# One ring of four double banks for the attention's PSUM tiles

## The chip, the cores and the metric

The kernel runs on one core of a Trainium2 chip. The metric is the device time of one execution in microseconds (us); lower is better. Inputs are the reference's arrays, the output is one float32 array of 8 x 576 x 512.

## What is computed

Attention over 8 batches and 8 heads with queries pooled by two, then a block that mixes tokens and channels:

```python
q_pool = q.reshape(B, H, S // 2, 2, D).mean(axis=3)          # 8, 8, 576, 64
scores = (1.0 / np.sqrt(D)) * np.matmul(q_pool, k.transpose(0, 1, 3, 2))
attn = np.exp(scores - np.max(scores, axis=-1, keepdims=True))
attn = attn / (np.sum(attn, axis=-1, keepdims=True) + 1e-09)
x = np.matmul(attn, v).transpose(0, 2, 1, 3).reshape(B, 576, 512)
theta = x @ w_theta
y = einsum('ts,bsd->btd', w_tok_r, x * cos(theta)) + einsum('ts,bsd->btd', w_tok_i, x * sin(theta))
u = x + y
out = u + np.maximum(u @ w_ch, 0.0)
```

q, k and v have 1152 rows of 64 per head.

## The kernel before

There are two parts, each with its own PSUM pool. The first makes x for all batches (attention), the second does the rest, batch by batch. The change touches the first part.

Attention goes over 32 pairs of heads (`NPAIR`), which overlap: while pair i is in its main stage, pair i+2 is in its maximum pass and pair i+3 is being prepared. The work of a pair:

- **Preparation** (`prep_t`, `prep_hi`, `prep_lo`, `prep_tail`; L252 to L292). TensorE transposes the keys and the pooled queries into a PSUM tile `pt` of two banks (L265), in two groups: g = 0 with six key blocks, g = 1 with the queries and three key blocks. ScalarE copies it, rounded, to `hi` (L281); VectorE writes the rest `lo` = `pt` - `hi` (L292), so that products can be made in three fast terms. For g = 1 ScalarE also copies the last 64 queries of both heads into a matrix `tail` (L288).
- **Maximum pass** (`maxpass`, L305 and L312). In twelve steps TensorE writes 128 queries by 384 keys for both heads to a tile `pm` (L305, 2 matmuls), and VectorE reduces it to a maximum (L312). The last 64 queries of both heads go together (`max_tail`): three matmuls fill the two banks of `px` (L322), and a fourth, of 128 columns, for which `px` has no room, goes to spare columns of another tile (L328; here called py's columns). VectorE reduces `px` (L331) and then py's columns (L332). `max_nm` (L337) and `max_row` (L342 to L344) turn the maxima into the row `mT`, which DMAs bring to `nmr` for the subtraction.
- **Main stage** (`escore`, L371 and L374). For each half u of the queries and each of nine key blocks TensorE makes a score tile `pe` (8 matmuls: four terms, two heads), and ScalarE writes its exponential to `pc` (L374). GpSimd adds these up (`ssum`, L383).
- **Output** (`av`, L392 and L399). 36 matmuls of `pc` and `vn` go to bank 0 of a tile `pa`, and ScalarE copies that to `xu`. The sums of the exponentials over the partitions go to bank 1 of the tile `pmt` (`norm_sum`, L408), and what follows divides by them.

Each PSUM tile of this part has two of the eight banks (`bank2`). In before there are two kinds with two tiles each: "e" for `pe` and `pa`, "m" for `pm`, `pt`, `px`, `pmt` and the transposed weights `pwt`. A new tile of a kind takes the place of the one two before it and waits until that has been read. The layer that records the program puts the semaphores in: instructions of different engines on one PSUM tile are kept in the order of the code, also where two only read it, and also, as the first matmul of L408 shows with the copy `mT` (L344), where they use different banks of it.

The order of the work on each engine is written out by hand: `plan` gives each step a position (18 score tiles of a pair are 18 units; `MAX_AT`, `AV_AT`, `W_AT` and `PLAN` are such positions), ties go by a priority, and each engine runs its instructions in that order. At `AV_AT` a pair has two bursts (`burst`): the first with the preparation of g = 1 for pair i+2, `max_row` and `av` for u = 0, the second with `tail_prep` and `av` for u = 1. In the second burst of before, the code has first the transposes of pair i+3, then `max_tail` of pair i+2, whose py's columns go to spare columns of the tile `pt` just transposed, then `hi` and `lo` of pair i+3, then `av`. Nine positions of a pair (`W_AT`) advance a generator by one step each; it narrows the weights of the second part, mostly on VectorE (L525 to L540), some steps on ScalarE and GpSimd.

Of the kernel before, what the change touches and what calls it, by code (L numbers as in the profile page):

```python
# [9 lines left out]
F32 = mybir.dt.float32  # L10
# [4 lines left out]
ALU = mybir.AluOpType  # L15
AX = mybir.AxisListType
# [1 line left out]
EPS = 1e-9  # L18
TAIL = 8
PC_BUFS = 14  # L20
MAX_AT = (-24.9, -23.65, -22.55, -20.85, -19.55, -18.8, -15.55, -14.35, -13.5, -11.6, -10.2, -9.15)
SS_LAG = 4.5
AV_AT = (10.35, 19.25)
W_FIRST = (9.45, 9.5, 9.85, 10.5, 12.75, 18.0, 18.6, 19.25, 20.45)
W_AT = (9.45, 9.5, 9.85, 10.5, 12.75, 18.0, 18.6, 19.25, 20.45)
W_LAST = (9.4, 10.2, 11.0, 11.8, 12.6, 13.4, 14.2, 15.0, 15.8, 16.6, 17.4, 18.2, 19.0, 19.8, 20.6, 21.4, 22.2, 23.0, 23.8, 24.6)
W_END = 30
PRO = ((-34.75, -25.8, -18.2), (-6.0, -5.0, 3.15), (3.75,))
MAX_AT0 = (-25.75, -25.25, -24.75, -24.25, -24.15, -23.25, -22.0, -21.95, -21.75, -21.25, -20.75, -20.25)
MAX_AT1 = (-18.1, -16.8, -16.1, -15.35, -14.7, -14.0, -13.3, -12.6, -11.7, -10.3, -9.8, -9.0)  # L30
PLAN = {
    "load_q": -44.55,
    "load_k": -43.2,
    "pool_q": -35.35,
    "load_max": -7.6,
    "load_v": -7.0,
    "max_nm": -8.85,
    "norm_spread": 29.0,
    "norm_load": 29.15,
    "norm_recip": 37.5,  # L40
    "norm_save": 37.6,
    "norm_bcast": 37.7,
# [2 lines left out]
}  # L45
MAN = ("PE", "Activation", "DVE", "Pool", "SP")
BANKS = {}
PAIRS = {"e": 2, "m": 2}
BANKS2 = {"h": 1, "t": 1, "m": 4, "r": 2}
MAN2 = ("PE", "Activation", "DVE", "Pool", "SP")  # L50
ENG2 = {'xlo0': 'vector', 'zlo0': 'gpsimd', 'xlo': 'gpsimd', 'zlo': 'gpsimd', 'ulo': 'vector'}
# [40 lines left out]
def pooled_attention_moe_kernel(  # L92
# [11 lines left out]
    nc = tc.nc  # L104
# [83 lines left out]
    with ExitStack() as p1:  # L188
# [63 lines left out]
        def prep_t(i, g):  # L252
            st = state[i]
            kn = st["kn"]
            pt = st["pt", g] = bank2("m", f"pt{g}_{i}")
            if g == 0:
                srcs = [[kn[:, t] for t in range(3 * n, 3 * n + 3)] for n in range(2)]
            else:
                qp = st["qp"]
                srcs = [[qp[:, t] for t in range(5)], [qp[:, 5]] + [kn[:, t] for t in (6, 7, 8)]]  # L260
            for n in range(2):
                c = 0
                for src in srcs[n]:
                    R = src.shape[0]
                    nc.tensor.transpose(  # L265
                        out=pt[:, n, c : c + R],
                        in_=src.rearrange("p h d -> p (h d)"),
                        identity=ident[0:R, 0:R],
                    )
                    c += R  # L270
# [12 lines left out]
        def prep_tail(i):  # L283
            st = state[i]
            tl = st["tail"] = tails[i % 2]
            c = QP - HT
            for hs in HEADS:
                nc.scalar.copy(tl[hs, hs], st["pt", 1][hs, 1, c : c + HT])  # L288
# [7 lines left out]
        def maxpass(i):  # L296
            st = state[i]
            hi = st["hi"]
            mx = st["mx"] = sml.tile([P, KT, 3], F32, tag="mx", name=f"mx{i}")
            W = 3 * P  # L300
            for j in range(4):
                for g in range(3):
                    pm = bank2("em"[g % 2] if i == 0 else "m", f"pm{i}_{j}{g}")
                    for h, hs in enumerate(HEADS):
                        nc.tensor.matmul(  # L305
                            pm[:, h, 0:W],
                            hi[hs, Q0 + j * P : Q0 + (j + 1) * P],
                            hi[hs, K0[3 * g] : K0[3 * g] + W],
                            start=True,
                            stop=True,  # L310
                        )
                    nc.vector.tensor_reduce(  # L312
                        mx[:, j : j + 5 : 4, g : g + 1], pm[:, :, 0:W], AX.X, ALU.max
                    )
                    yield

        def max_tail(i, pt):
            st = state[i]
            hi, tl, mx = st["hi"], st["tail"], st["mx"]
            pm = bank2("m", f"px{i}")  # L320
            for n, c, k, w in ((0, 0, 0, 4), (1, 0, 4, 2), (1, 2 * P, 6, 2)):
                nc.tensor.matmul(  # L322
                    pm[:, n, c : c + w * P], tl, hi[:, K0[k] : K0[k] + w * P], start=True, stop=True
                )
            st["pm", 0] = pm
            if pt is None:
                pt = bank2("m", f"py{i}")
            nc.tensor.matmul(  # L328
                pt[:, 0, 3 * P :], tl, hi[:, K0[8] : K0[8] + P], start=True, stop=True
            )  # L330
            nc.vector.tensor_reduce(mx[:, 8, 0:2], pm, AX.X, ALU.max)  # L331
            nc.vector.tensor_reduce(mx[:, 8, 2:3], pt[:, 0, 3 * P :], AX.X, ALU.max)  # L332
# [5 lines left out]

        def max_row(i):
            st = state[i]  # L340
            px = bank2("m", f"pmt{i}")
            nc.tensor.transpose(out=px[0:KT, 0, 0:P], in_=st["nm"], identity=ident)  # L342
            mT = st["mT"] = sml.tile([KT, P], F32R, tag="mT", name=f"mT{i}")
            nc.scalar.copy(mT, px[0:KT, 0, 0:P])  # L344
            return px
# [36 lines left out]
            first = st["pc"][u, 0] if kt == 1 else st["ss", u]  # L382
            nc.gpsimd.tensor_tensor(st["ss", u], first, st["pc"][u, kt], ALU.add)  # L383

        def av(i, u):
            st = state[i]
            if u == 0:
                st["xu"] = nrm.tile([P, 2, HALF], F32, tag="xu", name=f"xu{i}", bufs=3)
            pa = bank2("e", f"pa{i}_{u}")
            for kt in range(KT):  # L390
                for h, hs in enumerate(HEADS):
                    nc.tensor.matmul(  # L392
                        pa[hs, 0, 0:HALF],
                        st["vn"][:, h, kt, :],
                        st["pc"][u, kt][:, h, :],
                        start=(kt == 0),
                        stop=(kt == KT - 1),
                    )
            nc.scalar.copy(st["xu"][:, u, :], pa[:, 0, 0:HALF])  # L399
# [56 lines left out]
        def burst(i, u):  # L456
            if u == 0:
                if i + 2 < NPAIR:
                    prep_all(i + 2, 1)
                px = max_row(i + 1) if i + 1 < NPAIR else bank2("m", f"pmt{i}")  # L460
                av(i, u)
                if i > 0:
                    norm_sum(i - 1, px)
            else:
                tail_prep(i)
                av(i, u)

        def prep_all(i, g):
            if g == 0:
# [5 lines left out]
                prep_tail(i)  # L475

        def tail_prep(i):
            more = i + 3 < NPAIR
            if more:
                prep(i + 3)  # L480
                prep_t(i + 3, 0)
            if i + 2 < NPAIR:
                max_tail(i + 2, state[i + 3]["pt", 0] if more else None)
            if more:
                prep_hi(i + 3, 0)
                prep_lo(i + 3, 0)
# [9 lines left out]
        def weights():  # L496
# [494 lines left out]
```

## Time and profile before

| what | value |
|---|---|
| median of 3 timed runs | 1419.48 us (1417.49 to 1420.95) |
| the profiled execution | 1416.78 us, its span 1414.8 us |
| mean granted TensorE clock | 0.992 |
| busy share of the span: TensorE, its weight loads | 96%, 77% |
| VectorE, ScalarE, GpSimd | 61%, 52%, 64% |

The profile is of one execution. PE is TensorE's matmuls and PEld its weight loads, DVE is VectorE, ACT ScalarE, POOL GpSimd, SP the queue of the DMAs. Attention ends near 920 us. Times in rows are us from the span's start; "idle before" is how long an engine stood before a row and what released it. Matmul durations overlap: the next pair of matmuls starts before the last has drained, so the distance of two starts tells more than a duration.

### The profile page before, as it was taken

To read this page: it belongs to the slowest core of one execution; us is meant where nothing else is said; L and a number is where in the kernel's file an instruction comes from. 1 tells how busy PE (TensorE), PEld (TensorE's weight loads), DVE (VectorE), ACT (ScalarE), POOL (GpSimd) and SP (SyncE) were. 2 spreads that over 40 slices of the span, in tenths; PEclk is the share of its full clock that TensorE was granted. 3 is DMA by queue.
4 is the path that set the end of the run, shared out by engine and by line. 5 is a ranking of instruction groups with operands and counts; after the bars stand their busy time and mean duration, and the time that the engine had idled before them with its cause. 6 is when DMAs were issued, how large, how long until landed. Compare 5 with 4: busy or idle time off the path is not lost.

```text
span 1414.8 us, 29922 instructions
## 1 busy us (share of the span) xinstructions
PE 1352.8 (96%) x12178; PEld 1086.1 (77%) x12178; DVE 862.2 (61%) x1143; ACT 730.6 (52%) x1250; POOL 911.4 (64%) x672
## 2 busy tenths in 40 slices
PE   5999999999999999999999999999999999999998
PEld 4667676766676767767776766688999999999998
DVE  5866676777577767766687666355362553536442
ACT  2556465655555655556565655465444544445431
POOL 2789888978798889889898888834232413232210
PEclk7999999999999999999999999999999999999999
DMA  5224343434342443324343421231111211111111
GB/s 127 74 75 126 85 111 84 119 85 116 86 125 69 108 122 106 94 83 125 84 111 86 119 80 51 79 122 38 35 38 34 60 50 34 38 35 44 28 31 38
DMA packets 130906, 111.66 MB, mean 79 GB/s; under 512 B 95040, under 2 KB 95424, under 8 KB 130768
## 3 DMA queue, kind: packets, MB, share of 16 engines
q1 hardware_dynamic: 130592, 109.28, 28.0%
q8 instruction: 96, 1.57, 0.5%
q0 software_dynamic: 176, 0.46, 0.1%
q14 instruction: 42, 0.34, 0.1%
HBM read 88.29 MB, written 21.27 MB: 77 GB/s over the span
## 4 chain that ended last, share of the span: by engine, by line
PE 67%; DVE 15%; ACT 10%; DMA 3%; issue 3%; POOL 1%; SPq 0%; ACTq 0%; POOLq 0%; DVEq 0%
PE pa L392 16%; PE pe L371 16%; PE py L821 11%; PE pth L743 7%; PE pr L860 5%; DVE mx L312 5%; ACT pc L374 4%; PE pm L305 3%; PE pt L265 3%; PE pmt L408 2%; DMA kn<-in_k_dram 2%; DVE wf L532 1%; PE pxn L731 1%; DVE ws L530 1%; DVE lo L292 1%
## 5 line engine op out<-in xcount | busy, mean ns | idle before, releaser
L383 POOL TENSOR_TENSOR ss<-ss,pc 128x576 f32<-128x576 f32 x384 | 558.1, 1453 | 98.2 <-ACT pc L374 75.9
L312 DVE TENSOR_REDUCE mx<-pm 128x2 f32<-128x768 f32 x384 | 343.9, 950 | 134.8 <-PE pm L305 134.4
L374 ACT ACTIVATE pc<-pe 128x576 f32<-128x576 f32 x576 | 371.2, 652 | 102.2 <-PE pe L371 84.2
L392 PE MATMUL pa<-pc,vn 128*64 128x288 f32 x2304 | 293.5, 409 | 0.3 <-ACT pc L374 0.3
L794 POOL TENSOR_TENSOR Z<-ab,Z 128x512 fp32r<-128x512 f32 x40 | 52.2, 1305 | 306.0 <-ACT Z L790 277.8
L392 PEld LDWEIGHTS pa<-pc,vn 128*64 128x64 f32 x2304 | 159.7, 137 | 110.7 <-ACT pc L374 4.8
L821 PE MATMUL py<-wtk,Z 128*128 128x288 f32 x1728 | 241.7, 297 | 0.0
L821 PEld LDWEIGHTS py<-wtk,Z 128*128 128x128 f32 x1728 | 233.2, 189 | 1.3
L371 PE MATMUL pe<-hi 64*128 64x288 f32 x1152 | 203.1, 349 | 14.9 <-ACT pc L374 6.5
L371 PEld LDWEIGHTS pe<-hi 64*128 64x128 f32 x1152 | 108.3, 184 | 92.9 <-ACT pc L374 57.9
L371 PE MATMUL pe<-hi,lo 64*128 64x288 f32 x1152 | 170.8, 293 | 0.0
L371 PE MATMUL pe<-lo,hi 64*128 64x288 f32 x1152 | 170.8, 293 | 0.0
L371 PE MATMUL pe<-nmr,oner 64*128 64x288 f32 x1152 | 169.5, 290 | 0.0
L305 PE MATMUL pm<-hi 64*128 64x384 f32 x768 | 138.1, 359 | 14.6 <-DVE mx L312 8.6
L371 PEld LDWEIGHTS pe<-lo,hi 64*128 64x128 f32 x1152 | 109.8, 187 | 0.0
L371 PEld LDWEIGHTS pe<-hi,lo 64*128 64x128 f32 x1152 | 109.1, 186 | 0.0
L371 PEld LDWEIGHTS pe<-nmr,oner 64*128 64x128 f32 x1152 | 109.0, 185 | 0.0
L292 DVE TENSOR_TENSOR lo<-pt,hi 128x768 fp32r<-128x768 f32 x64 | 67.6, 1057 | 66.9 <-ACT hi L281 66.9
L860 PEld LDWEIGHTS pr<-us,wch 128*128 128x128 f32 x768 | 104.5, 188 | 2.0
L860 PE MATMUL pr<-us,wch 128*128 128x288 f32 x768 | 105.8, 295 | 0.0
L281 ACT CAST hi<-pt 128x768 fp32r<-128x768 f32 x64 | 56.2, 878 | 91.5 <-DVE mx L332 74.3
L383 POOL TENSOR_TENSOR ss<-pc,pc 128x576 f32<-128x576 f32 x64 | 93.8, 1466 | 3.0 <-ACT pc L374 3.0
(105 smaller groups left out, 1652.7 us busy)
## 6 DMA issues: line engine op xcount, KB each, us to landing
qn<-in_q_dram SPq DMA_DIRECT2D x32, 576.0 KB
kn<-in_k_dram SPq DMA_DIRECT2D x64, 288.0 KB
vn<-in_v_dram SPq DMA_DIRECT2D x32, 576.0 KB
dn<-ro SPq DMA_DIRECT2D x64, 144.0 KB
xd<-xu SPq DMA_DIRECT2D x32, 288.0 KB
xT<-xd SPq DMA_DIRECT2D x8, 1152.0 KB
out_dram<-on SPq DMA_DIRECT2D x23, 192.0 KB
out_dram<-on SPq DMA_DIRECT2D x23, 128.0 KB
```

The source lines that it names most:

```text
L281: nc.scalar.copy(hi, src)
L292: nc.vector.tensor_tensor(lo, src, hi.bitcast(F32), ALU.subtract)
L305: nc.tensor.matmul(pm[:, h, 0:W], hi[hs, Q0 + j * P : Q0 + (j + 1) * P], hi[hs, K0[3 * g] : K0[3 * g] + W], start=True, stop=True,)
L312: nc.vector.tensor_reduce(mx[:, j : j + 5 : 4, g : g + 1], pm[:, :, 0:W], AX.X, ALU.max)
L371: nc.tensor.matmul(pe[:, h, 0:HALF], w[hs], x[hs], start=(n == 0), stop=(n == 3))
L374: nc.scalar.activation(pcs[u, kt], pe[:, :, 0:HALF], AF.Exp, scale=SC)
L383: nc.gpsimd.tensor_tensor(st["ss", u], first, st["pc"][u, kt], ALU.add)
L392: nc.tensor.matmul(pa[hs, 0, 0:HALF], st["vn"][:, h, kt, :], st["pc"][u, kt][:, h, :], start=(kt == 0), stop=(kt == KT - 1),)
L743: nc.tensor.matmul(th, xs[c][:, j * P : (j + 1) * P], ws[:, c], start=(n == 0), stop=(n == 11))
L794: engine("zlo", b).tensor_tensor(Z[1], t, Z[0].bitcast(F32), ALU.subtract)
L821: nc.tensor.matmul(st["py", c, u][:, 0:HALF], Z[zi][:, c * P : (c + 1) * P], wtk[wi][:, kw, u * HALF : (u + 1) * HALF], start=(i == 0 and ...
L860: nc.tensor.matmul(pr[u][:, 0:HALF], wch[wi][:, c, e * P : (e + 1) * P], st["us", ui][:, c, u * HALF : (u + 1) * HALF], start=(n == 0), st ...
```

## The change

There is one kind of tile, "e", with four tiles in a ring (the same eight banks): every tile waits for the one four before it, whichever of `pe`, `pm`, `pt`, `px`, `pmt`, `pwt` and `pa` that is. `tail` is copied from `hi` in SBUF rather than from `pt`; `hi` holds the same rounded values. In the second burst `hi` and `lo` of pair i+3 come right behind the transposes in the code, then the tile `pa` of u = 1 is taken, py's columns go to its bank 1, and `av` writes its bank 0. Positions of many steps move by small amounts. Of these the three that the prediction names: the weight step at 10.5 goes to 9.896, ahead of the first burst; the one at 19.25, which stood behind the second burst, is at 19.246, ahead of it (19.269); and the one at 20.45 goes to 19.685.

```diff
-MAX_AT = (-24.9, -23.65, -22.55, -20.85, -19.55, -18.8, -15.55, ...)
+MAX_AT = (-24.792, -23.501, -21.909, -20.702, -19.409, -18.667, -15.437, ...)
-AV_AT = (10.35, 19.25)
+AV_AT = (10.348, 19.269)
-W_AT = (9.45, 9.5, 9.85, 10.5, 12.75, 18.0, 18.6, 19.25, 20.45)
+W_AT = (9.455, 9.493, 9.833, 9.896, 12.767, 17.992, 18.599, 19.246, 19.685)
...
-PAIRS = {"e": 2, "m": 2}
+PAIRS = {"e": 4}
...
         def prep_t(i, g):
-            pt = st["pt", g] = bank2("m", f"pt{g}_{i}")
+            pt = st["pt", g] = bank2("e", f"pt{g}_{i}")
...
         def prep_tail(i):
-            c = QP - HT
+            c = Q0 + SQ - HT
             for hs in HEADS:
-                nc.scalar.copy(tl[hs, hs], st["pt", 1][hs, 1, c : c + HT])
+                nc.scalar.copy(tl[hs, hs], st["hi"][hs, c : c + HT].bitcast(F32))
...
         def maxpass(i):
-                    pm = bank2("em"[g % 2] if i == 0 else "m", f"pm{i}_{j}{g}")
+                    pm = bank2("e", f"pm{i}_{j}{g}")
...
         def max_tail(i, pt):
-            pm = bank2("m", f"px{i}")
+            pm = bank2("e", f"px{i}")
...
             nc.tensor.matmul(
-                pt[:, 0, 3 * P :], tl, hi[:, K0[8] : K0[8] + P], start=True, stop=True
+                pt[:, 1, 0:P], tl, hi[:, K0[8] : K0[8] + P], start=True, stop=True
             )
             nc.vector.tensor_reduce(mx[:, 8, 0:2], pm, AX.X, ALU.max)
-            nc.vector.tensor_reduce(mx[:, 8, 2:3], pt[:, 0, 3 * P :], AX.X, ALU.max)
+            nc.vector.tensor_reduce(mx[:, 8, 2:3], pt[:, 1, 0:P], AX.X, ALU.max)
...
-        def av(i, u):
+        def av(i, u, pa=None):
...
-            pa = bank2("e", f"pa{i}_{u}")
+            if pa is None:
+                pa = bank2("e", f"pa{i}_{u}")
...
         def burst(i, u):
...
             else:
-                tail_prep(i)
-                av(i, u)
+                av(i, u, tail_prep(i))
...
         def tail_prep(i):
-            more = i + 3 < NPAIR
-            if more:
-                prep(i + 3)
-                prep_t(i + 3, 0)
+            if i + 3 < NPAIR:
+                prep_all(i + 3, 0)
+            pa = bank2("e", f"pa{i}_1")
             if i + 2 < NPAIR:
-                max_tail(i + 2, state[i + 3]["pt", 0] if more else None)
-            if more:
-                prep_hi(i + 3, 0)
-                prep_lo(i + 3, 0)
+                max_tail(i + 2, pa)
+            return pa
```

Behind L386 the numbers of after are higher by one, behind L474 lower by three: L393 is before's L392, L529 its L532.

The built order shows three places. Names carry the pair's number, so `pt0_12` is `pt` of pair 12, group 0, and `pa9_1` is `pa` of pair 9, u = 1; the last number is the tile's. In brackets are the counters that an instruction waits for.

TensorE at the second burst of pair 9, before and then after:

```order
L265 MATMUL pt0_12_4156<-ident_63,kn12_4009 128x128 [waits DMAHW6_49,DMAHW5_49,DVE_49]
L265 MATMUL pt0_12_4156<-ident_63,kn12_4009 128x128 x5
L322 MATMUL px11_4163<-hi11_3766,tail_1_113 128x512 [waits DVE_49]
L322 MATMUL px11_4163<-hi11_3766,tail_1_113 128x256 x2
L328 MATMUL pt0_12_4156<-hi11_3766,tail_1_113 128x128
L392 MATMUL pa9_1_4172<-pc9_10_3922,vn9_3634 64x288 [waits Activation_49]
L392 MATMUL pa9_1_4172<-pc9_10_3922,vn9_3634 64x288
```

```order
L265 MATMUL pt0_12_4159<-ident_63,kn12_4009 128x128 [waits DMAHW6_49,DMAHW5_49,Activation_49]
L265 MATMUL pt0_12_4159<-ident_63,kn12_4009 128x128 x5
L322 MATMUL px11_4169<-hi11_3768,tail_1_113 128x512 [waits DVE_49]
L322 MATMUL px11_4169<-hi11_3768,tail_1_113 128x256 x2
L328 MATMUL pa9_1_4168<-hi11_3768,tail_1_113 128x128 [waits Activation_49]
L393 MATMUL pa9_1_4168<-pc9_10_3922,vn9_3634 64x288 [waits DVE_49]
L393 MATMUL pa9_1_4168<-pc9_10_3922,vn9_3634 64x288
```

py's columns (L328) have gone from `pt0_12` to `pa9_1`, and the first product of `pa9_1` waits for VectorE instead of ScalarE. Of VectorE's instructions only the reduction of py's columns touches that tile.

VectorE at the second burst of pair 12, where weight steps (`wf`, `raw`) stand, before and then after:

```order
L532 TENSOR_SCALAR wf_5112<-ws_5107 128x576 [waits DVE_49]
L536 SCALAR_TENSOR_TENSOR wf_5112<-raw_5108,wf_5112 128x576 [waits DVE_49]
L331 TENSOR_REDUCE mx14_5201<-px14_5338 128x2 [waits PE_49]
L332 TENSOR_REDUCE mx14_5201<-pt0_15_5331 128x1 [waits PE_49]
L292 TENSOR_TENSOR lo15_5330<-pt0_15_5331,hi15_5329 128x768 [waits Activation_49]
L540 TENSOR_SCALAR raw_5108<-wf_5112 128x576 [waits DVE_49]
```

```order
L529 TENSOR_SCALAR wf_5112<-ws_5106 128x576 [waits DVE_49]
L533 SCALAR_TENSOR_TENSOR wf_5112<-raw_5107,wf_5112 128x576 [waits DVE_49]
L537 TENSOR_SCALAR raw_5107<-wf_5112 128x576 [waits DVE_49]
L292 TENSOR_TENSOR lo15_5331<-pt0_15_5332,hi15_5330 128x768 [waits Activation_49]
L331 TENSOR_REDUCE mx14_5201<-px14_5342 128x2 [waits PE_49]
L332 TENSOR_REDUCE mx14_5201<-pa12_1_5341 128x1 [waits PE_49]
```

`lo15` has gone from behind the two reductions to ahead of them, and a third weight step stands ahead of it. In the whole program 29 second bursts have `lo` in this place; 8 of them have three weight operations ahead of it in after, 3 have two.

TensorE between two score tiles in the first half of pair 10's second set of score tiles, before and then after:

```order
L305 MATMUL pm12_02_4451<-hi12_4154 128x384 [waits DVE_49]
L305 MATMUL pm12_02_4451<-hi12_4154 128x384
L371 MATMUL pe10_15_4456<-hi10_3381 128x288 [waits Activation_49]
L371 MATMUL pe10_15_4456<-hi10_3381 128x288
L371 MATMUL pe10_15_4456<-lo10_3382,hi10_3381 128x288 x2
L371 MATMUL pe10_15_4456<-hi10_3381,lo10_3382 128x288 x2
L371 MATMUL pe10_15_4456<-nmr_0_108,oner_116 128x288 x2
L371 MATMUL pe10_16_4469<-hi10_3381 128x288 [waits Activation_49]
```

```order
L371 MATMUL pe10_15_4452<-hi10_3382 128x288 [waits DVE_49]
L371 MATMUL pe10_15_4452<-hi10_3382 128x288
L371 MATMUL pe10_15_4452<-lo10_3383,hi10_3382 128x288 x2
L371 MATMUL pe10_15_4452<-hi10_3382,lo10_3383 128x288 x2
L371 MATMUL pe10_15_4452<-nmr_0_108,oner_116 128x288 x2
L305 MATMUL pm12_02_4462<-hi12_4157 128x384 [waits Activation_49]
L305 MATMUL pm12_02_4462<-hi12_4157 128x384
L371 MATMUL pe10_16_4469<-hi10_3382 128x288 [waits DVE_49]
```

The maximum tile `pm12_02` has gone one score tile back; `pe10_15` and `pe10_16` wait for VectorE (the reductions of maximum tiles) where they waited for ScalarE's exponentials, and the maximum tile the other way round.

More of the change, by code (lines that the diff above doesn't have):

```diff
@@ L20 @@
 PC_BUFS = 14
-MAX_AT = (-24.9, -23.65, -22.55, -20.85, -19.55, -18.8, -15.55, -14.35, -13.5, -11.6, -10.2, -9.15)
-SS_LAG = 4.5
-AV_AT = (10.35, 19.25)
-W_FIRST = (9.45, 9.5, 9.85, 10.5, 12.75, 18.0, 18.6, 19.25, 20.45)
-W_AT = (9.45, 9.5, 9.85, 10.5, 12.75, 18.0, 18.6, 19.25, 20.45)
+MAX_AT = (-24.792, -23.501, -21.909, -20.702, -19.409, -18.667, -15.437, -14.192, -13.369, -11.488, -10.057, -9.003)
+SS_LAG = 4.342
+AV_AT = (10.348, 19.269)
+W_FIRST = (9.455, 9.493, 9.833, 10.5, 12.767, 17.992, 18.599, 19.246, 20.453)
+W_AT = (9.455, 9.493, 9.833, 9.896, 12.767, 17.992, 18.599, 19.246, 19.685)
 W_LAST = (9.4, 10.2, 11.0, 11.8, 12.6, 13.4, 14.2, 15.0, 15.8, 16.6, 17.4, 18.2, 19.0, 19.8, 20.6, 21.4, 22.2, 23.0, 23.8, 24.6)
 W_END = 30
-PRO = ((-34.75, -25.8, -18.2), (-6.0, -5.0, 3.15), (3.75,))
-MAX_AT0 = (-25.75, -25.25, -24.75, -24.25, -24.15, -23.25, -22.0, -21.95, -21.75, -21.25, -20.75, -20.25)
-MAX_AT1 = (-18.1, -16.8, -16.1, -15.35, -14.7, -14.0, -13.3, -12.6, -11.7, -10.3, -9.8, -9.0)
+PRO = ((-34.735, -25.8, -18.218), (-6.497, -4.34, 3.145), (3.732,))
+MAX_AT0 = (-25.726, -25.226, -24.726, -24.226, -24.163, -23.745, -21.992, -21.972, -21.726, -21.226, -20.726, -20.226)
+MAX_AT1 = (-18.123, -16.8, -16.1, -15.375, -14.7, -14.0, -13.3, -12.6, -11.714, -10.295, -9.8, -8.999)
 PLAN = {
-    "load_q": -44.55,
-    "load_k": -43.2,
-    "pool_q": -35.35,
+    "load_q": -44.542,
+    "load_k": -43.209,
+    "pool_q": -35.622,
     "load_max": -7.6,
     "load_v": -7.0,
-    "max_nm": -8.85,
+    "max_nm": -8.851,
     "norm_spread": 29.0,
-    "norm_load": 29.15,
+    "norm_load": 29.426,
     "norm_recip": 37.5,
@@ L326, in max_tail @@
             if pt is None:
-                pt = bank2("m", f"py{i}")
+                pt = bank2("e", f"py{i}")
             nc.tensor.matmul(
-                pt[:, 0, 3 * P :], tl, hi[:, K0[8] : K0[8] + P], start=True, stop=True
+                pt[:, 1, 0:P], tl, hi[:, K0[8] : K0[8] + P], start=True, stop=True
             )
             nc.vector.tensor_reduce(mx[:, 8, 0:2], pm, AX.X, ALU.max)
-            nc.vector.tensor_reduce(mx[:, 8, 2:3], pt[:, 0, 3 * P :], AX.X, ALU.max)
+            nc.vector.tensor_reduce(mx[:, 8, 2:3], pt[:, 1, 0:P], AX.X, ALU.max)
         def max_nm(i):
@@ L340, in max_row @@
             st = state[i]
-            px = bank2("m", f"pmt{i}")
+            px = bank2("e", f"pmt{i}")
             nc.tensor.transpose(out=px[0:KT, 0, 0:P], in_=st["nm"], identity=ident)
@@ L459, in burst @@
                     prep_all(i + 2, 1)
-                px = max_row(i + 1) if i + 1 < NPAIR else bank2("m", f"pmt{i}")
+                px = max_row(i + 1) if i + 1 < NPAIR else bank2("e", f"pmt{i}")
                 av(i, u)
@@ L584, in token @@
                 yield
-                pw2 = bank2("m", "pwt")
+                pw2 = bank2("e", "pwt")
                 pt = pw2[:, 0]
@@ L685, in pooled_attention_moe_kernel @@
             plan(i)
-        at(NU * NPAIR + 2, 9, lambda: norm_sum(NPAIR - 1, bank2("m", "pend")))
+        at(NU * NPAIR + 2, 9, lambda: norm_sum(NPAIR - 1, bank2("e", "pend")))
         pw = ExitStack()
```

## The prediction

> **What bounds the kernel now.** I read the page first. The profiled execution took 1416.78 us, its span is 1414.8 us, so 2.0 us lie around it; the median of the three timed runs, 1419.48, is 2.7 us above the profiled one.
>
> ```profile
> span 1414.8 us, 29922 instructions
> PE 1352.8 (96%) x12178; PEld 1086.1 (77%) x12178; DVE 862.2 (61%) x1143; ACT 730.6 (52%) x1250; POOL 911.4 (64%) x672
> ```
>
> Then the windows of 50 us. A row gives, after the window's length, the busy time of PE, PEld, DVE, ACT and POOL, the granted clock, the DMA share and GB/s.
>
> ```profile
> 300.00:350.00 50.00, 47.07 (x502) 34.96 (x494) 35.00 (x39) 29.03 (x48) 44.53 (x33) 1.00 0.44 117
> 1050.00:1100.00 50.00, 49.69 (x344) 47.06 (x343) 21.13 (x37) 22.71 (x38) 15.45 (x11) 1.00 0.10 25
> ```
>
> The first is attention, which the change touches, the second is the part behind it, which it leaves alone. TensorE is the engine in use in both, but in attention it loses some 3 us of 50. Whatever makes TensorE stand still there lengthens the kernel; whatever lets it run on shortens it. So the timeline of one pair comes next (start, duration, engine, line; idle time and its releaser in brackets), in a stretch of score products:
>
> ```profile
> 300.62 0.40 PE L371 MATMUL pe<-hi 64*128 64x288 f32 x2
> 302.23 0.19 PEld L371 LDWEIGHTS pe<-hi 64*128 64x128 f32 x2 [0.20 <-ACT pc L374]
> 302.23 0.40 PE L371 MATMUL pe<-hi 64*128 64x288 f32 x2
> 302.47 0.30 PE L371 MATMUL pe<-lo,hi 64*128 64x288 f32 x2
> 302.87 0.33 PE L305 MATMUL pm<-hi 64*128 64x384 f32 x2
> 303.04 0.30 PE L371 MATMUL pe<-hi 64*128 64x288 f32 x2
> 303.13 1.35 ACT L374 ACTIVATE pc<-pe 128x576 f32<-128x576 f32 x2 [0.25 <-PE pe L371]
> 303.83 0.19 PEld L371 LDWEIGHTS pe<-hi 64*128 64x128 f32 x2 [0.34 <-ACT pc L374]
> ```
>
> Two score tiles take 1.61 us (302.23 to 303.84), though ScalarE's two exponentials take 1.35 and TensorE waits 0.2 to 0.34 in each turn. With two score tiles in PSUM, TensorE writes the next one only when the exponential two before has been read. The second place is the burst in which a pair's second output half is made:
>
> ```profile
> 307.56 0.29 PE L371 MATMUL pe<-nmr,oner 64*128 64x288 f32 x2
> 307.95 0.65 ACT L374 ACTIVATE pc<-pe 128x576 f32<-128x576 f32 x1 [0.22 <-PE pe L371]
> 308.50 0.84 PE L265 MATMUL pt<-ident,kn 128*128 128x128 f32 x6 [0.65 <-DMA kn<-in_k_dram]
> 309.10 0.71 PE L322 MATMUL px<-hi,tail 128*128 128x512 f32 x3
> 309.64 0.22 PE L328 MATMUL pt<-hi,tail 128*128 128x128 f32 x1
> 309.80 4.59 PE L392 MATMUL pa<-pc,vn 128*64 128x288 f32 x36
> 309.84 1.23 DVE L331 TENSOR_REDUCE mx<-px 128x2 f32<-128x1024 f32 x1 [2.30 <-PE px L322]
> 310.99 0.28 DVE L332 TENSOR_REDUCE mx<-pt 128x1 f32<-128x128 f32 x1
> 311.30 0.80 ACT L281 CAST hi<-pt 128x768 fp32r<-128x768 f32 x1 [2.70 <-DVE mx L332]
> 312.13 0.96 DVE L292 TENSOR_TENSOR lo<-pt,hi 128x768 fp32r<-128x768 f32 x1 [0.87 <-ACT hi L281]
> ```
>
> TensorE goes from the tail's last columns (309.64) straight into `pa` (309.80). The whole train behind them, both reductions, `hi` and `lo`, runs from 309.84 to 313.09 beside the 4.59 us of `pa` and costs nothing. The waits, by pair of engines (total us, times, longest), say the same for the kernel:
>
> ```profile
> ACT hi L281 <- DVE mx L332: 74.3, 29, 4.6
> PEld pe L371 <- ACT pc L374: 57.9, 196, 1.2
> ACT tail L288 <- DVE lo L292: 53.7, 32, 4.5
> PEld pe L371 <- issue: 27.6, 66, 0.5
> PEld pm L305 <- DVE mx L312: 15.9, 25, 1.6
> PE pm L305 <- DVE mx L312: 8.6, 21, 1.3
> PEld pmt L408 <- ACT mT L344: 7.3, 7, 2.1
> PE pmt L408 <- ACT mT L344: 3.8, 6, 1.6
> ```
>
> The two long waits of ScalarE are those that the change removes, but both lie under a burst; the waits on TensorE's side are what a ring can win.
>
> **The change part by part.**
>
> *The last columns in the result tile.* This adds a wait on TensorE. `py`'s columns now go into bank 1 of the tile `pa`, VectorE reduces them there (L332), and the first product of `pa` carries a wait on VectorE's counter. VectorE has touched nothing else of that tile, so the wait is for L332. That two banks of one tile are kept apart in this way the trace of before shows: the sums of L408 write bank 1 of `pmt` while the copy `mT` reads bank 0, and they wait for it (3.8 us in the last row above).
>
> What is queued behind that wait is all of TensorE: 36 matmuls of `pa`, then the next score tiles. And the code now has `lo` ahead of the two reductions on VectorE, so the wait covers the whole train, worked out from the rows of the burst, with py's start (309.64) as zero. The transposes end at -0.30 and the last exponential in a pair without the `kn` wait at about -0.35, so `hi` starts at about -0.2 and ends at 0.6 (0.80); `lo` 0.65 to 1.6 (0.96); the two reductions take 1.43 (309.84 to 311.27), to 3.05; TensorE starts some 0.1 later, at 3.15. Before it started at 0.16. Stall 3.0 us. Bounds: 2.4 if `hi` and `lo` come half a microsecond sooner, 3.4 with the mean durations. `hi` waited for L332 29 times (the first of the waits above), once in each burst with this train: 29 x 3.0 = 87 us (70 to 99). Nothing hides it: ScalarE has no exponential left to do, and the 0.2 to 0.34 us waits later in the pair come from the turn-around of two tiles, not from a backlog that a pause would clear.
>
> *Weight steps ahead of lo.* The third weight step at 19.246 now stands ahead of the burst (19.269). In the built order 8 of the 29 bursts have three weight operations on VectorE ahead of `lo`, 3 have two. A burst with two before:
>
> ```profile
> 391.28 2.69 DVE L312 TENSOR_REDUCE mx<-pm 128x2 f32<-128x768 f32 x3
> 393.88 1.22 DVE L532 TENSOR_SCALAR wf<-ws 128x576 uint32<-128x576 uint32 x1
> 395.13 2.40 DVE L536 SCALAR_TENSOR_TENSOR wf<-raw,wf 128x576 uint32<-128x576 uint32 x1
> 395.36 0.22 PE L328 MATMUL pt<-hi,tail 128*128 128x128 f32 x1
> 397.45 1.21 DVE L331 TENSOR_REDUCE mx<-px 128x2 f32<-128x1024 f32 x1
> ```
>
> And the shortest of the steps, from the groups by line (busy us, mean ns):
>
> ```profile
> L540 DVE TENSOR_SCALAR raw<-wf 128x512 uint32<-128x512 uint32 (+2 forms) x18 | 12.5, 697 | 0.2
> ```
>
> Two take 3.6 us, from 393.88 to 397.45, a third 0.7 (L540) to 1.2 (as L532) more, so `lo` could start at 398.1 to 398.7. Without them, 0.65 after py's start, which in this burst is 395.36, it would start at 396.0. The stall grows by 2.1 to 2.7: 8 x 2.4 = 19 us. Two steps alone end at 397.45, up to 1.4 late, less where the shorter ones stand: 3 x 0.7 = 2 us. Together 21 (10 to 35).
>
> *The ring.* Where score and maximum tiles alternate strictly, four in one ring are the same two and two, and nothing changes. Where two score tiles follow each other, the later one now waits for a reduction that ended long ago, and the maximum tile behind it for the exponential. I followed nine score tiles through with the rows above: 0.133 us from one matmul pair to the next (302.47 to 302.87 in three), 0.24 for the first after a wait (302.23 to 302.47), 0.17 for a maximum tile (302.87 to 303.04), 0.29 and 0.1 until ScalarE starts, 0.68 per exponential, 0.90 per reduction (three in 2.69, below). Zero is 300.62, the half's first tile, 12. Its exponential ends at 1.58; tile 14 waits for that as before and stands until 2.25. Tile 15 needs only the first reduction (1.92) and ends at 2.78, the maximum tile at 2.95, tile 16 at 3.48, without the wait for exponential 14 (3.19). Tile 17 waits for exponential 15 (3.87) and ends at 4.54, 18 with its maximum tile at 5.26; 00 waits for exponential 17 (5.48) and ends at 6.15, 01 at 6.68. Before it ended at 7.07 (307.69): 0.4 sooner. The second half, where the maximum tiles stand one place earlier, gives 0.6 by the same walk: there only waits of under 0.1 are left. 1.0 us a pair; I take 0.8, since score tiles now also wait for VectorE where a weight step stands between reductions: 30 x 0.8 = -24 us. Bounds: 0, if these waits eat it, and -95 if all of the 57.9, 27.6 and 8.6 us above went.
>
> *Tail copies from SBUF.* They no longer stand behind `lo` at the head of ScalarE's queue, so `mT` and the four row loads behind it come sooner. Of this only the 3.8 + 7.3 us of L408 are on TensorE: -6 (0 to -11).
>
> *VectorE freed later in the pair.* The third weight step is gone from the second half, so some of the 15.9 + 8.6 us of L305 goes: -8 (0 to -20). The `kn` load is issued from the same place and comes no sooner: 0. The small moves of other positions shift no row by more than one score tile: 0 (-3 to +3).
>
> Sum: 1416.8 + 87 + 21 - 24 - 6 - 8 = 1486.8, and 2.7 for the median: 1489.5, rounded to 1490.
>
> **The rivals.**
>
> *The clock falls in the stalls.* At the start of the kernel the trace has a stretch at half clock:
>
> ```profile
> 15.00:20.00 5.00, 3.27 (x12) 1.58 (x12) 5.00 (x7) 0.00 (x0) 0.00 (x0) 0.50 0.42 112
> 32.90 0.44 PE L371 MATMUL pe<-hi,lo 64*128 64x288 f32 x2
> 33.13 0.44 PE L371 MATMUL pe<-nmr,oner 64*128 64x288 f32 x2
> 36.84 0.44 PE L305 MATMUL pm<-hi 64*128 64x384 f32 x2 [1.26 <-DVE mx L331]
> ```
>
> There a matmul pair follows after 0.23 instead of 0.134 us. A gap of 1.26 us once it is warm did not bring it down again, and no longer one stands later in attention: the trace can't say what 3.0 us do. If each stall cost about 5 us at half clock, 0.44 of it is lost, 2.2 x 29 = 64: 1555. If only the 8 long stalls did, 18: 1508. Chance of the whole 0.15. The Trainium skill (TensorE: Matmul & The Clock Gate, Why this matters for your kernels) speaks against this change here: no idle gaps over some 3 us between bursts, or the clock halves. By its window of about 3.4 us the plain stalls just escape and those of some 5.5 us can be caught; no row of before shows it.
>
> *The ring wins nearly all of the waits.* Then -95 instead of -24: 1419. For it: the waits on ScalarE are the largest of TensorE's. Against it: in alternating order the distance is the same. Halfway, -60, gives 1454. Chance 0.1 for a gain that large.
>
> *Faster.* The wait on VectorE is met early, because it is for an older operation, or `pa` does not depend on it. Then 1416.8 - 24 - 6 - 8 + 2.7 = 1381. It decides at the point where the train of `hi`, `lo` and two reductions ends before py's columns are written plus the gains of a pair: below 1.3 us (38 us in 29 bursts) instead of 3.0. A wait of that length would need `lo` behind the reductions, as in the code of before. The Trainium skill (PSUM — Partial Sum Buffer, PSUM bank collisions raise a hardware error) has only accesses to one bank collide, and these are two; the hardware would not need the wait. But the program carries it. Chance 0.05. That the change does nothing, all waits gone and new ones equal, is the end of the ring's rival, 0.02.
>
> **How the numbers follow.** Forecast, with its bounds 1450 to 1520: 0.68; clock 0.15; ring 0.1; faster 0.05; same 0.02. A measurement of this kernel tells 0.2% (2.8 us) from no change. The range takes in the ring's half and most of the clock's case: 1440 to 1540. Faster 0.05, same 0.02, slower 0.93.
>
> **What would show it.** Right: a wait "PE pa <- DVE mx" at the line of `pa`'s products, 29 times, 80 to 110 us in all, at most near 6; `lo` ahead of the reduction of `px`; ScalarE's waits for L332 and for `lo` gone; "PEld pe <- ACT pc" down by a third to a half. Clock: window rows in attention under 1.00. Wrong: `pa` starting within 1.3 us of the tail's columns, or an attention part that is no longer than before.

## The result and the profile after

The change makes the kernel slower: 1552.13 us median (1549.89 to 1556.91, 4 runs) against 1420.22 us, a ratio of 1.0945 with a 95% interval of 1.0925 to 1.0965. 1490 us was predicted with 1440 to 1540: the direction is right, the time lies above the range, next to the rival that put the clock's fall at 1555. The profiled execution took 1556.91 us, 140.1 more than the profiled one of before.

The page of after, its first rows and the rows of three groups (busy us, mean ns of one, then the idle time ahead of them):

```profile
span 1555.1 us, 29872 instructions
PE 1393.1 (90%) x12178; PEld 1108.9 (71%) x12178; DVE 870.3 (56%) x1143; ACT 727.8 (47%) x1250; POOL 912.4 (59%) x672
...
L393 PE MATMUL pa<-pc,vn 128*64 128x288 f32 x2304 | 350.4, 467 | 127.7 <-DVE mx L332 126.7
L371 PEld LDWEIGHTS pe<-hi 64*128 64x128 f32 x1152 | 108.7, 184 | 68.7 <-issue 29.2
L305 PE MATMUL pm<-hi 64*128 64x384 f32 x768 | 135.9, 351 | 3.9 <-ACT hi L281 2.1
```

Two numbers of the first group carry the loss. TensorE stood 126.7 us ahead of `pa`, waiting for the reduction L332, where before it stood 0.3. And the same 2304 matmuls are busy for 350.4 us instead of 293.5, 56.9 us more. Together 183.6 us; the span grew by 140.3, so 43.3 us were won elsewhere; the idle time of the weight loads of `pe` is 24.2 us less (92.9 before), that of `pm` 10.7 less (14.6 before).

The burst of one pair, all engines with the score tiles left out (start, duration, engine, line):

```profile
90.60 0.85 PE L265 MATMUL pt<-ident,kn 128*128 128x128 f32 x6
91.20 0.71 PE L322 MATMUL px<-hi,tail 128*128 128x512 f32 x3
91.48 0.80 ACT L281 CAST hi<-pt 128x768 fp32r<-128x768 f32 x1 [0.18 <-PE pt L265]
91.75 0.22 PE L328 MATMUL pa<-hi,tail 128*128 128x128 f32 x1
92.32 0.96 DVE L292 TENSOR_TENSOR lo<-pt,hi 128x768 fp32r<-128x768 f32 x1 [1.74 <-ACT hi L281]
93.19 1.22 DVE L331 TENSOR_REDUCE mx<-px 128x2 f32<-128x1024 f32 x1
94.32 0.28 DVE L332 TENSOR_REDUCE mx<-pa 128x1 f32<-128x128 f32 x1
...
94.66 6.28 PE L393 MATMUL pa<-pc,vn 128*64 128x288 f32 x36 [2.69 <-DVE mx L332]
```

Read it as a chain: transposes, `hi`, `lo`, two reductions, then `pa`. The train that ran beside `pa` before now stands ahead of it, and TensorE does nothing from 91.97 to 94.66. Then the 36 matmuls take 6.28 us where they took 4.59. The windows of the same place show why (PE, PEld, DVE, ACT, POOL busy, then the granted clock):

```profile
91.97:94.66 2.69, 0.00 (x2) 0.00 (x1) 2.34 (x4) 0.31 (x1) 2.69 (x3) 1.00 0.30 75
94.66:96.66 2.00, 2.00 (x10) 1.09 (x12) 0.06 (x1) 0.00 (x0) 1.92 (x3) 0.55 0.52 176
96.66:98.66 2.00, 2.00 (x14) 1.02 (x12) 0.00 (x0) 0.00 (x0) 0.93 (x1) 0.60 0.26 58
98.66:100.66 2.00, 2.00 (x20) 1.07 (x16) 0.00 (x0) 0.00 (x0) 0.00 (x0) 1.00 0.83 234
```

TensorE is busy in all three windows behind the stall, but at half clock for 3.4 us: the granted clock falls at 94.84 and is full again at 98.26. A busy engine is not a fast one: only the clock's column tells.

Not all stalls are of 2.7 us. VectorE's rows of the longest:

```profile
157.49 1.43 DVE L522 TENSOR_SCALAR raw<-raw 128x576 uint32<-128x576 uint32 x1 [5.90 <-DMA raw<-in_moe_w_tok_r_dram]
158.84 0.94 DVE L292 TENSOR_TENSOR lo<-pt,hi 128x768 fp32r<-128x768 f32 x1
159.71 1.21 DVE L331 TENSOR_REDUCE mx<-px 128x2 f32<-128x1024 f32 x1
160.84 0.28 DVE L332 TENSOR_REDUCE mx<-pa 128x1 f32<-128x128 f32 x1
```

py's columns were written at 152.7. A weight step (before's L525) stood at the head of VectorE's queue until its weights had come from memory, with `lo`, both reductions and, through them, TensorE behind it: 8.26 us. The trace has four such steps, each ahead of `lo` in a second burst:

```profile
DVE raw L522 <- DMA raw<-in_moe_w_tok_r_dram: 5.9, 1, 5.9
DVE raw L522 <- DMA raw<-in_moe_w_tok_i_dram: 4.4, 1, 4.4
DVE raw L522 <- DMA raw<-in_moe_w_ch_dram: 4.0, 1, 4.0
DVE raw L522 <- DMA raw<-in_moe_w_theta_dram: 3.1, 1, 3.1
```

### The profile page after: what moved, and what is told of

Same layout as the page of the kernel before. It is cut to its first block, busy times and chain, and to the rows that moved or that the text cites. A ratio compares the mean times of both kernels' runs of the same rounds, so it can differ in the third digit from the quotient of the medians.

```text
span 1555.1 us, 29872 instructions
## 1 busy us (share of the span) xinstructions
PE 1393.1 (90%) x12178; PEld 1108.9 (71%) x12178; DVE 870.3 (56%) x1143; ACT 727.8 (47%) x1250; POOL 912.4 (59%) x672
## 4 chain that ended last, share of the span: by engine, by line
PE 67%; DVE 18%; ACT 6%; DMA 4%; issue 2%; POOL 2%; SPq 0%; ACTq 0%; POOLq 0%; DVEq 0%
PE pa L393 21%; PE pe L371 15%; PE py L818 10%; PE pth L740 6%; DVE mx L312 5%; PE pr L857 5%; PE pm L305 3%; PE pt L265 3%; DVE mx L331 2%; PE pmt L409 2%; DVE lo L292 2%; DMA kn<-in_k_dram 1%; ACT pc L374 1%; PE pxn L728 1%; ACT hi L281 1%
## 5 line engine op out<-in xcount | busy, mean ns | idle before, releaser
L312 DVE TENSOR_REDUCE mx<-pm 128x2 f32<-128x768 f32 x384 | 343.9, 952 | 296.1 <-PE pm L305 295.9
L393 PE MATMUL pa<-pc,vn 128*64 128x288 f32 x2304 | 350.4, 467 | 127.7 <-DVE mx L332 126.7
L374 ACT ACTIVATE pc<-pe 128x576 f32<-128x576 f32 x576 | 366.3, 652 | 74.4 <-PE pe L371 54.9
L393 PEld LDWEIGHTS pa<-pc,vn 128*64 128x64 f32 x2304 | 184.5, 157 | 272.9 <-DVE mx L332 131.1
L400 ACT COPY xu<-pa 128x288 f32<-128x288 f32 x64 | 25.6, 400 | 390.3 <-PE pa L393 390.3
```

The source lines that it names most:

```text
L312: nc.vector.tensor_reduce(mx[:, j : j + 5 : 4, g : g + 1], pm[:, :, 0:W], AX.X, ALU.max)
L374: nc.scalar.activation(pcs[u, kt], pe[:, :, 0:HALF], AF.Exp, scale=SC)
L393: nc.tensor.matmul(pa[hs, 0, 0:HALF], st["vn"][:, h, kt, :], st["pc"][u, kt][:, h, :], start=(kt == 0), stop=(kt == KT - 1),)
```

## The experiments

The theory after the result: py's columns in `pa`'s tile make TensorE wait for VectorE, and the idle time makes it slow afterwards; ring and tail copies are gains. The rivals: the ring or the positions cost something; `pa` is slow for a reason other than the clock.

**py's columns back in `pt`.** After with this part undone, `hi` and `lo` behind the reductions again:

```diff
-                pt[:, 1, 0:P], tl, hi[:, K0[8] : K0[8] + P], start=True, stop=True
+                pt[:, 0, 3 * P :], tl, hi[:, K0[8] : K0[8] + P], start=True, stop=True
...
-                av(i, u, tail_prep(i))
+                tail_prep(i)
+                av(i, u)
```

> After with one part undone: py's columns go to the spare columns of pt, and hi and lo stand behind the reductions, as before; ring, tail copies and positions are after's. If the wait of pa's first product for L332, and the slow matmuls behind it, are the whole loss, TensorE goes from py's columns to pa within 0.3 us again, and the time is 1416.8 - 38 + 2.7 = 1381 us (1365 to 1400), faster than before. If the ring, the tail copies or the positions cost something, it stays above 1420.

1397.25 us, ratio to before 0.9849 (0.9830 to 0.9869). All of the loss is gone, and ring, tail copies and positions together are a gain of 22 us. In the burst `pa` follows at once, at full clock:

```profile
83.86 0.22 PE L328 MATMUL pt<-hi,tail 128*128 128x128 f32 x1
84.01 4.59 PE L393 MATMUL pa<-pc,vn 128*64 128x288 f32 x36
84.06 1.23 DVE L331 TENSOR_REDUCE mx<-px 128x2 f32<-128x1024 f32 x1 [1.42 <-PE px L322]
```

The gain is smaller than the 38 us of the prediction. A wait appears that before did not have, of score tiles for a late `lo`:

```profile
PE pe L371 <- DVE lo L292: 16.1, 12, 1.6
```

**Work inside the stall.** After with matmuls that nothing uses, behind py's columns:

```diff
             nc.tensor.matmul(
                 pt[:, 1, 0:P], tl, hi[:, K0[8] : K0[8] + P], start=True, stop=True
             )
+            for _ in range(11 if i >= 2 else 0):
+                nc.tensor.matmul(
+                    pt[:, 1, P:], tl, hi[:, K0[0] : K0[0] + 3 * P], start=True, stop=True
+                )
```

> After with 11 more matmuls of 128x384 behind py's columns, into columns of pa's second bank that nothing reads: about 2.2 us of work that no one uses, inside the stall. VectorE reaches L332 only 2.6 us after py's columns, so pa starts when it did. If the matmuls of pa after a stall are slow because an idle TensorE loses its clock, pa takes 4.5 us again instead of 6.2 in the 18 or so plain bursts, 18 x 1.7 = 31 us less: 1521 us, and the long stalls of 5.3 us and more, which keep 3 us of idle time, show whether that is enough to lose it. If pa is slow for another reason (its tile, or what ScalarE and GpSimd do beside it), the time stays at 1552 us or goes above it.

1525.51 us, ratio to before 1.0753 (1.0737 to 1.0769): 27 us faster than after, with more work. `pa` starts no sooner; it runs faster:

```profile
91.70 0.22 PE L328 MATMUL pa<-hi,tail 128*128 128x128 f32 x1
91.76 2.13 PE L332 MATMUL pa<-hi,tail 128*128 128x384 f32 x11
94.61 4.59 PE L397 MATMUL pa<-pc,vn 128*64 128x288 f32 x36 [0.72 <-DVE mx L336]
```

All 18 bursts whose idle time fell to between 0.6 and 1.6 us take 4.6 us again; the 12 that keep 3.8 us or more take 6.0 to 7.6. So the slowness belongs to the idle time, and not to the tile or to what other engines do beside it.

The same with 4 matmuls:

> After with 4 unused matmuls of 128x384 behind py's columns instead of 11: about 0.8 us of work, so the plain stalls keep about 1.9 us of idle time. With 2.7 us idle nearly every burst behind ran slow, with 1.45 one of some 17, with 0.7 none. If idle time itself sets it, part of the plain bursts run slow here: between 1525 and 1552 us. If anything under 2.7 us is free, all of them take 4.5 us: 1523 us.

One run, 1546.87 us, with 1416 to 1422 for before beside it. `pa` stays slow in 8 of the 10 bursts with 1.8 to 2.0 us of idle time:

```profile
90.47 0.92 PE L332 MATMUL pa<-hi,tail 128*128 128x384 f32 x4
93.32 6.28 PE L397 MATMUL pa<-pc,vn 128*64 128x288 f32 x36 [1.93 <-DVE mx L336]
```

**Reductions first.** After with `hi` and `lo` of pair i+3 behind the reductions, py's columns still in `pa`:

```diff
-            if i + 3 < NPAIR:
-                prep_all(i + 3, 0)
+            more = i + 3 < NPAIR
+            if more:
+                prep(i + 3)
+                prep_t(i + 3, 0)
             pa = bank2("e", f"pa{i}_1")
             if i + 2 < NPAIR:
                 max_tail(i + 2, pa)
+            if more:
+                prep_hi(i + 3, 0)
+                prep_lo(i + 3, 0)
             return pa
```

> After with hi and lo of pair i+3 behind the two reductions in the code; py's columns stay in pa. If the train ahead of L332 sets the stall, a plain one falls from 2.7 to about 1.5 us and a long one by 0.9: 32 us less. If the clock falls in a stall of 2.7 us but not in one of 1.5, another 18 x 1.7 = 31 us go: 1489 us. If a stall of 1.5 us loses the clock too: 1520 us. If lo's place does not matter: 1552 us.

1500.10 us, ratio to before 1.0576 (1.0559 to 1.0594), 52 us faster than after. The plain stall is at most 1.46 us and 13 of the 14 `pa` behind it run at full clock:

```profile
91.13 0.22 PE L328 MATMUL pa<-hi,tail 128*128 128x128 f32 x1
91.33 1.23 DVE L331 TENSOR_REDUCE mx<-px 128x2 f32<-128x1024 f32 x1 [1.35 <-PE px L322]
92.47 0.28 DVE L332 TENSOR_REDUCE mx<-pa 128x1 f32<-128x128 f32 x1
92.81 4.59 PE L393 MATMUL pa<-pc,vn 128*64 128x288 f32 x36 [1.46 <-DVE mx L332]
...
L393 PE MATMUL pa<-pc,vn 128*64 128x288 f32 x2304 | 326.8, 443 | 93.6 <-DVE mx L332 92.6 <-PE pmt L342 1.0
```

The waits fall by 34.1 us (126.7 to 92.6; 32 expected), the busy time by 23.6 (350.4 to 326.8; 31 expected). Both halves of the loss answer to the length of the train.

**The third weight step behind the burst.** After with one position moved:

```diff
-W_AT = (9.455, 9.493, 9.833, 9.896, 12.767, 17.992, 18.599, 19.246, 19.685)
+W_AT = (9.455, 9.493, 9.833, 9.896, 12.767, 17.992, 18.599, 19.3, 19.685)
```

(the same in `W_FIRST`)

> After with the third weight step at 19.3, behind the second burst as in before, instead of 19.246. If VectorE's weight steps ahead of lo make the long stalls, 8 bursts lose about 1.4 us each and the three with a weight step that waits for its data 3 to 5 us each: 24 us less, 1528 us. If they only take the place of another wait: 1545 to 1552 us.

1526.96 us, ratio to before 1.0762 (1.0745 to 1.0778), 25 us faster than after, as expected. The waits ahead of `pa` fall by 29.6 us, the slow matmuls hardly change:

```profile
L393 PE MATMUL pa<-pc,vn 128*64 128x288 f32 x2304 | 347.2, 464 | 98.1 <-DVE mx L332 97.1 <-PE pmt L342 1.0
```

**The suspected part alone.** Before with py's columns in `pa` and `hi` and `lo` ahead of the reductions (the code of after in `tail_prep`, `av`, `burst` and `max_tail`); two kinds of tiles, tail copies and positions as before:

> Before with py's columns in pa's second bank and hi and lo ahead of the reductions, and nothing else: two kinds of two tiles, before's tail copies and positions. If this alone makes the loss: two weight steps ahead of lo as in the run with the third one behind the burst, so about 97 us of stalls and 54 us of slow matmuls, and none of the ring's gain: 1419 + 151 = 1570 us. If the ring is needed for it, far less: under 1500 us.

1560.08 us, ratio to before 1.0994 (1.0969 to 1.1020). This part alone costs 142 us:

```profile
L393 PE MATMUL pa<-pc,vn 128*64 128x288 f32 x2304 | 346.4, 463 | 89.9 <-DVE mx L332 89.6 <-ACT pc L374 0.3
```

89.6 of waits and 52.9 of slow matmuls make 142.5. The ring is not needed for the loss.

**The ring alone.** Before with the one ring:

```diff
-PAIRS = {"e": 2, "m": 2}
+PAIRS = {"e": 4}
```

and "m" replaced by "e" wherever a tile is taken.

> Before with the ring of four alone; tail copies, py's columns, lo's place and all positions are before's. The prediction's term for the ring is -24 us: 1395 us. The run with py's columns back in pt showed 22 us less for ring, tail copies and positions together; if those come from the ring alone it is 1397 us; if from the tail copies, the ring alone gives 1415 us or no gain.

1410.46 us, ratio to before 0.9946 (0.9929 to 0.9963): -8 us, a third of the term. The waits of `pe`:

```profile
PEld pe L371 <- DVE mx L312: 30.7, 69, 1.5
PEld pe L371 <- ACT pc L374: 19.6, 93, 0.5
PE pe L371 <- DVE mx L312: 16.9, 24, 1.3
```

Of 57.9 us for the exponentials 38.3 are gone, but 30.7 us for VectorE's reductions came in their place: a score tile that no longer waits for ScalarE now waits for a VectorE that is as late.

**The tail copies alone.** Before with this edit:

```diff
-            c = QP - HT
+            c = Q0 + SQ - HT
             for hs in HEADS:
-                nc.scalar.copy(tl[hs, hs], st["pt", 1][hs, 1, c : c + HT])
+                nc.scalar.copy(tl[hs, hs], st["hi"][hs, c : c + HT].bitcast(F32))
```

> Before with the tail copies from SBUF alone. The prediction's term is -6 us: 1413 us, with the waits of L408 for the copy mT gone. If those waits come from elsewhere (the maxima of a late VectorE), 1419 us.

1405.15 us, ratio to before 0.9907 (0.9890 to 0.9923): -13 us, twice the term. The waits of L408 for `mT` are gone, as expected. What the prediction set at nothing, the wait for the `kn` load, shrank too, from 12.4 us in 8 places to

```profile
PE pt L265 <- DMA kn<-in_k_dram: 8.0, 2, 7.7
```

where 7.7 is the first load of the kernel: the row loads that start with `mT` stand ahead of `kn` on the DMA queue, and both are issued sooner. These two make 8 of the 13 us (3.8 and 4.4). The waits of the weight loads of `pe` for the exponentials fell too, from 57.9 to 48.6 us; how much of the other 5 us is theirs was not followed.

**py's columns in `pt` and the third weight step behind the burst.** The first experiment's kernel with that step at 19.3.

> After with py's columns back in pt, hi and lo behind the reductions, and the third weight step behind the second burst (19.3). With py's columns back alone it was 1397 us, with a new wait of score tiles for lo of 16 us in 12 places, all behind weight steps. If the third step makes lo late, most of those 16 us go: 1385 us (1381 was forecast for a change without stall). If not: 1397 us.

1397.41 us, ratio to before 0.9849 (0.9830 to 0.9869): no gain over 1397.25. The wait for `lo` went, and the maximum tiles waited instead (17.0 us where it was 2.4):

```profile
PE pm L305 <- DVE mx L312: 17.0, 19, 2.4
```

**A tile of its own for py's columns.** After with `hi` and `lo` still ahead of the reductions:

```diff
-            pa = bank2("e", f"pa{i}_1")
             if i + 2 < NPAIR:
-                max_tail(i + 2, pa)
-            return pa
+                max_tail(i + 2, None)
```

> After with one edit: py's columns get a tile of their own in the ring, so pa's first product has nothing of VectorE's to wait for; hi and lo stay ahead of the reductions, and the third weight step ahead of the burst. If the shared tile is the cause, the stalls (127 us) and the slow matmuls behind them (57 us) go: 1552 - 184 = 1368 us at best, 1368 to 1400, since the second half of a pair then meets a VectorE that is late. If lo's place ahead of the reductions or the positions are the cause, it stays above 1450 us.

1389.54 us, ratio to before 0.9793 (0.9777 to 0.9809): 163 us faster than after, by one tile. The train is the one of after, but `pa` no longer waits for it. Of later score tiles six wait for `lo`, 6.4 us in all and 3.2 once, behind a weight step that starts after 6.5 us of waiting:

```profile
84.03 0.22 PE L328 MATMUL py<-hi,tail 128*128 128x128 f32 x1
84.18 4.59 PE L393 MATMUL pa<-pc,vn 128*64 128x288 f32 x36
84.59 0.96 DVE L292 TENSOR_TENSOR lo<-pt,hi 128x768 fp32r<-128x768 f32 x1 [1.68 <-ACT hi L281]
85.47 1.21 DVE L331 TENSOR_REDUCE mx<-px 128x2 f32<-128x1024 f32 x1
86.60 0.28 DVE L332 TENSOR_REDUCE mx<-py 128x1 f32<-128x128 f32 x1
```

With the third weight step at 19.3 as well:

> The same with the third weight step behind the second burst (19.3). If late weight steps are what TensorE meets in the second half, 5 us less than the run with py's own tile; if not, the same. With py in pt the move gave nothing (1397.3 and 1397.4 us).

1385.53 us, ratio to before 0.9772 (0.9757 to 0.9786). This is the fastest version of the study, 2.3% under before.

Where the pairs' time goes, from the timelines: the mean length, over 25 pairs from the fourth on, of the parts between the first matmuls on TensorE (us; the first burst; first half's score tiles; transposes to py's columns; py's columns to `pa`; `pa`; second half's score tiles; preparation to the next pair; sum):

```
                      burst  half 1  to py  stall   pa   half 2  prep   sum
before                 6.02   7.57   1.23   0.15   4.54   7.45   0.95  27.92
ring alone             6.15   7.41   1.19   0.17   4.58   7.34   0.88  27.72
tail copies alone      5.85   7.37   1.24   0.15   4.54   7.43   0.95  27.54
after                  5.89   6.97   1.19   4.50   6.43   6.76   0.88  32.63
py back in pt          5.87   7.01   1.18   0.15   4.52   7.65   0.88  27.27
py's own tile          5.86   6.93   1.20   0.30   4.80   7.06   0.88  27.03
own tile, step moved   5.92   6.95   1.20   0.24   4.54   7.09   0.88  26.83
```

A part lasts until the next one's first matmul, so `pa` of the row of py's own tile (4.80) holds the waits for `lo` behind it.

After wins 0.60 us in the first half and 0.69 in the second. The second of these is not the ring's own: with py's columns back in `pt` it is gone (7.65), and with a tile of their own 0.39 of it is left (7.06). The likely reason, which no run shows by itself, is that without the stall VectorE comes into that half with work undone; then the stall pays for part of the gain that stands against it.

The positions were not tried alone. Ring and tail copies alone give 8 and 13 us, and with the positions 22; if the gains add up, the positions are worth little.

## Why the prediction was wrong

- *The added wait*: right in place, cause and engine. The plain stall is 2.7 us (3.0 worked out), there are 30 waits (29 forecast), and ScalarE's waits for L332 and `lo` are gone as forecast; the suspected part alone gives the loss, and a tile of its own for py's columns takes it away.
- *Bursts with weight steps*: the mechanism was right, the term too small. The eight triples stall 5.9 us on average, 3.2 more than the plain ones (2.4 predicted), and four bursts stall 5.4, 6.9, 6.9 and 8.3, since a weight step waits for its data there; the prediction had no term for that, although VectorE's waits for the weights were in the trace of before. Together 126.7 us instead of 108.
- *The clock*: this is the step that failed. The forecast let the matmuls behind a stall run at full clock and gave a fall in every stall 0.15, on the ground that a gap of 1.26 us had not brought it down. The fall came behind 29 of the 30 stalls and costs 56.9 us (64 in the rival's price, 1.5 to 2.9 a stall instead of 2.2; its rows, 0.134 us against 0.23, give a loss of 0.42 and not 0.44, so 2.1 a stall). Filling the stall with unused work brought 27 us back, so idle time is the cause. The Trainium skill (TensorE: Matmul & The Clock Gate, Part 1) has the clock halve after an idle window of about 3.4 us; here stalls of 1.9 us were mostly enough.
- *The ring*: 24 us was far too much for the ring alone (8 us). The walk had VectorE's reductions on time, but they were not: the row of before with 15.9 and 8.6 us of waits for L312 said so. In after more came out: the waits for the exponentials fell from 57.9 to 14.8 us, where a third to a half was forecast, likely because the stall let VectorE catch up: the weight loads of `pe` wait 5.3 us for its reductions there and 30.7 with the ring alone.
- *Tail copies*: -13 instead of -6. The prediction had seen that the row loads come sooner and not that `kn` stands behind them on the same queue; it put `kn` at nothing.
- *VectorE freed later in the pair* (-8): the waits of `pm` for L312 did fall, from 15.9 and 8.6 us to 6.2 and 1.4, but not for the reason given. With the ring alone, the third step where it was, they are 7.3 and 2.4, and moving that step back behind the burst cost nothing without the stall (1397.25 to 1397.41, and 1389.54 to 1385.53).
- *The sum*: the measured terms are 126.7 us of waits, 56.9 of slow matmuls and -43.3 for all the rest, which is what remains of the growth of 140.3 and was not measured by itself. Forecast were 108, 0 and -38. The clock's term is the largest error; the stalls give 19 us more.
- *Faster*, the rival in which `pa` does not wait, gave 1381 and is what a tile of its own does: 1389.5 and 1385.5.

The trace of before could say more about the clock than the prediction took from it. The stretch at half clock at the kernel's start was read as the state before TensorE is warm, but it begins with a fall. Two gaps, of 1.05 and 1.26 us, lie close together there:

```profile
11.87 0.80 PE L305 MATMUL pm<-hi 64*128 64x384 f32 x6 [1.05 <-ACT hi L281]
13.92 0.90 PE L305 MATMUL pm<-hi 64*128 64x384 f32 x4 [1.26 <-DVE mx L312]
```

The windows of the same place have full clock until 14.08 and half clock from there (third number from the end):

```profile
10.66:14.08 3.42, 1.11 (x9) 0.63 (x10) 2.64 (x4) 1.37 (x3) 1.96 (x2) 1.00 0.54 122
14.08:34.56 20.48, 14.78 (x77) 11.13 (x78) 16.01 (x20) 4.38 (x8) 3.51 (x4) 0.50 0.40 102
```

Nor was 1.26 us the longest gap of attention that did no harm: one of 1.64 us stands ahead of `pmt` at 385.71. So the length of a single gap was the wrong measure; the last section has a better one.

## What to carry to other kernels

Before a small result goes into spare room of a tile, ask who reads it, what stands ahead of that reader in its queue, and which engine writes the same tile next: here one reduction of 0.28 us put a train of 2.7 us and more, four times with the wait for a DMA in it, ahead of the busiest engine. Price a stall of TensorE with the matmuls behind it too. Take a threshold for it from a run and not from the longest gap that happened to do no harm, and add up the gaps that lie close together. A gain that is found together with a stall has to be measured without it.

## What the runs showed of the hardware

TensorE's clock falls after less idle time than expected. By the idle time directly ahead of `pa` and the length of `pa` (4.6 us at full clock, about 6 or more else): with 0.6 to 1.6 us all of 18 bursts kept the clock (11 unused matmuls); with 1.1 to 1.5 us 13 of 14 (reductions first); with 1.8 to 2.0 us 2 of 10 (4 unused matmuls); with 2.6 to 3.1 us 1 of 15 (after). The length of a stall alone does not decide: single bursts kept the clock with 2.15 us (reductions first), 2.29 (4 unused matmuls) and 2.67 (after), and one lost it with 1.46.

What decides between equal stalls can be read from the traces. In all 13 of them every change of the granted clock comes a whole number of 3.41 us after the one before: in after, half clock lasts 3.41, 6.83 or 10.24 us behind the stalls, and full clock mostly 27.31. So the changes lie on a grid of 3.41 us. Two stalls of after, of 2.67 and 2.68 us, show what it does. Their rows are steps of the grid; the first number behind the comma is TensorE's busy time, the third from the end the clock:

```profile
483.97:487.38 3.41, 1.65 (x16) 1.28 (x12) 1.71 (x3) 1.89 (x3) 3.33 (x4) 1.00 0.42 145
487.38:490.79 3.41, 2.50 (x22) 1.50 (x24) 1.49 (x4) 0.00 (x0) 2.75 (x2) 1.00 0.03 1
514.69:518.10 3.41, 0.73 (x8) 0.54 (x7) 2.40 (x4) 0.80 (x1) 3.41 (x5) 1.00 0.03 3
518.10:521.51 3.41, 3.41 (x16) 1.75 (x18) 0.01 (x1) 0.00 (x0) 3.33 (x3) 0.50 0.14 28
```

The first stall is cut in two by a step's end: 1.76 us of idle time in one step, 0.91 in the next, and the clock stays. The second lies in one step with 2.68 us, and the clock falls at the end of that step. Over all 13 traces the clock fell 158 times, always behind a step with 1.76 us of idle time or more; of the 5041 steps at full clock without a fall behind them none had more than 1.85. So on this kernel a step of 3.41 us that is idle for some 1.8 us, in one gap or several, costs the clock. The fall at the start of before fits: 1.05 and 1.26 us in one step. The clock came back only behind a step with less than 0.8 us of idle time. Behind a plain stall of 2.7 us that mostly takes one step, and `pa` takes 6.28 us instead of 4.59. This was read from the traces afterwards; no run moved a stall along the grid on purpose.
